# Attention and two MLPs on one core: the first two pairs of heads issued in the written order, the first weight read from GpSimd's queue

## The chip, the cores and the metric

One core of a Trainium2 chip runs the kernel. Its engines are TensorE (PE in the profile: matrix products into PSUM), VectorE (DVE), ScalarE (ACT), GpSimd (POOL) and SyncE (SP, which here only issues DMAs). Each issues its own instructions strictly in order and waits on the others by semaphores. The metric is the device time of one execution in microseconds (us). The kernel before takes 930.9 us, the median of three runs (930.15 to 1106.56).

## The reference

Causal attention on 4 batches of 8 heads, 576 positions, head size 64, with a bias from running sums of max(s, 0), then two MLPs on the 2304 tokens of width 512, each up to 2048 and back:

```python
scores = q @ k.T / sqrt(64)
cum = cumsum(max(s, 0)); scores += min(-(cum[:, None] - cum[None, :]), 0)
attn = softmax(where(causal, -1e9, scores)); y = attn @ v
x = y.transpose(0, 2, 1, 3).reshape(2304, 512)
x = max(x @ w1_in, 0) ** 2 @ w1_out
h = x @ w2_in; out = max(0.01 * h, h) @ w2_out
```

## The kernel before, in words

Heads are worked two at a time: a `Pair` holds two heads on the upper and lower 64 partitions, and there are 16 pairs, four to a batch. A pair has seven slots (`STEPS`, line 78): the score tiles of 128 query rows, kinds 0 (tiles 0 and 1), 2 and 3 once for each head, and kind 4, the last 64 rows of both heads. In a slot VectorE takes a tile's scores plus mask from PSUM and reduces them to the row minimum (`maxima`, line 488; on the reversed sign, so it is the maximum), ScalarE takes the exponential with the row sum (line 512), TensorE transposes the result (`flip`, line 527), ScalarE (kinds 0 and 2, line 550) or VectorE (kinds 3 and 4, line 548) copies that out of PSUM as `pT`, TensorE multiplies by the values (`values`, line 569), ScalarE copies the product to `xo` (line 579), and VectorE scales it by the inverse of the sums (lines 585, 586 and 610, with a broadcast `ex` made by GpSimd, line 589, and turned by TensorE, line 604). TensorE makes the scores of a coming tile (lines 469 and 457) as soon as their PSUM banks, tagged `S` and `h`, are free. The next pair's q and k are transposed by VectorE (line 427; from pair 5 on also split into two parts, lines 430 to 432).

Two other streams are laid into these slots. From slot 35 (the start of pair 5) TensorE works on the first MLP's first product (`up1`, line 661, called by `fill`), for blocks of 512 tokens whose attention is done. From slot 11, at the pace of one for 2.5 slots, `load_w` makes the 16 pieces of the first weight ready: a read of 512 KB of "words" by DMA (line 154) into one of two buffers `wst`, two ScalarE steps (lines 114 and 115), two VectorE steps (117 and 120), a sum on GpSimd (122), then the rounded copy (169 on ScalarE, or 171 on VectorE) and the rest on GpSimd (172). Each `yield` ends the part of one slot.

What sets the order: the program is written slot by slot (lines 810 to 867), and a scheduler that plays the program on a clock of its own may issue each engine's instructions in another order, where nothing ties them. `in_order(start, engines)` ties all instructions of the named engines since `start` to the order in which they are written. Before, one such tie covers TensorE from slot 35 to the end; shorter ones cover single groups of TensorE.

Of the kernel before, what the change touches and what calls it, by code (L numbers as in the profile page):

```python
# [18 lines left out]
def f32(ap):  # L19
    return ap.bitcast(F32)  # L20
# [3 lines left out]
def attention_then_two_mlps(  # L24
# [24 lines left out]
    nc = tc.nc  # L49
# [61 lines left out]
    def words(t, st, adder=nc.gpsimd):  # L111

        lw, hw = st[:, :, 0], st[:, :, 1]
        nc.scalar.activation(f32(t), f32(hw), AF.Copy, scale=2.0 ** -112)  # L114
        nc.scalar.activation(lw, lw, AF.Copy, scale=2.0 ** -29)  # L115
        yield
        nc.vector.tensor_scalar(t, t, 0x07FFFFFF, 3, ALU.bitwise_and, ALU.logical_shift_left)  # L117
        if adder is nc.vector:
            nc.vector.tensor_tensor(t, t, lw, ALU.add)  # L119
        nc.vector.scalar_tensor_tensor(t, hw, 0xC0000000, t, ALU.bitwise_and, ALU.bitwise_or)  # L120
        if adder is not nc.vector:
            adder.tensor_tensor(t, t, lw, ALU.add)
        yield
# [25 lines left out]
    def read_w(st, w, ch, rows, queue=nc.sync):  # L149

        if rows:
            queue.dma_start(st.rearrange("p f t -> p (f t)"), w.bitcast(U32)[ch * P:(ch + 1) * P, :])
        else:
            queue.dma_start(
                st.rearrange("p (c f) t -> p c (f t)", c=KC),
                w.bitcast(U32)[:, ch * 2 * P:(ch + 1) * 2 * P].rearrange("(c p) f -> p c f", p=P))

    def load_w(fc, pool, stage, lo_engine=nc.gpsimd):

        st = stage.words()  # L160
        read_w(st, w1_in, fc, False)
        for _ in range(3):
            yield
        dst = pool.tile([P, 2, DM], F32R, tag=f"w{fc}", name=f"w{fc}")
        win[fc] = dst
        t = stage.word()
        yield from words(t, st)
        if fc < 10:
            nc.scalar.activation(dst[:, 0], f32(t), AF.Copy)
        else:  # L170
            nc.vector.tensor_copy(dst[:, 0], f32(t))
        lo_engine.tensor_tensor(dst[:, 1], f32(t), f32(dst[:, 0]), ALU.subtract)
# [143 lines left out]
    def in_order(start, engines):  # L316

        before = {}
        for i in nc.cur_bb.bb.instructions[start:]:
            if i.engine not in engines:  # L320
                continue
            if i.engine in before:
                tc.add_manual_dep(
                    i, before[i.engine].name,
                    mybir.DependencyInfo(mybir.DependencyClass.NoSync, mybir.DependencyReason.DATA),
                    reason="in_order")
            before[i.engine] = i
# [180 lines left out]
    def exponentials(t, m, tiles, sums, c0):  # L508

        for x, (a, z, c) in enumerate(tiles):  # L510
            s0 = c0 + 2 * x
            done = nc.scalar.activation(t[:, a:z], t[:, a:z], AF.Exp, bias=m[:, c:c + 1], scale=-1.0,  # L512
                                        accum_out=sums[:, s0:s0 + 1])
        return done.ins
# [156 lines left out]
    def attention(at, mg, mx):  # L671

        n = len(STEPS)
# [3 lines left out]
        def at_slot(y, f, *args):  # L677
            later.setdefault(y, []).append((f, args))
# [51 lines left out]
        START = [4 * n * (j + 1) + (10 if j else 7) for j in range(B)]  # L730
# [6 lines left out]
        for x in range(len(pairs)):  # L737
            y = n * x
# [18 lines left out]
        stage = Stage(at, at, 2)  # L757
        for fc in range(FC):
            job = load_w(fc, wpool, stage)
            for gap in range(6):  # L760
                at_slot(CV + 5 * fc // 2 + (4 if fc > 7 else 0) + gap, step, job)
        for ch in range(BEFORE):
            job = convert(*divmod(ch, FC), stage, nc.sync, 3)
# [45 lines left out]
        live, anchors = {}, [None, None]  # L809
        for y in range(end + 14):  # L810
            x, st = divmod(y, n)
            if y == START[0]:
                fixed_from = len(nc.cur_bb.bb.instructions)
            if y < end:
                args = maxima(at, x, *STEPS[st])
                live[y] = args[0]
                behind = [args[-1], exponentials(*args[:-1])]
# [357 lines left out]
```

## Time and profile before

| | us |
|---|---|
| median of 3 runs (lowest, highest) | 930.9 (930.15, 1106.56) |
| the profiled execution | 932.79 |
| its span, first to last instruction | 931.0 |
| busy: PE, DVE, ACT, POOL | 898.3, 705.7, 577.7, 179.9 |
| first reduction of pairs 0 to 4 (line 488) | 10.69, 22.63, 34.78, 49.43, 64.81 |
| first product of `up1` (line 661) | 78.70 |

A row of the timeline gives start, duration, engine, line, operation, and in brackets how long the engine stood idle before it and what released it. A row of the windows gives a stretch (start:end), its length, then the busy time and number of instructions of PE, PE's weight loads, DVE, ACT and POOL, the granted clock of TensorE as a share of its full speed, the busy share of the DMA engines, and GB/s. A row of the waits gives who waited for whom, us in total, times, and the longest.

### The profile page before, as it was taken

What the parts mean: (1) busy time and instruction counts of PE and PEld (TensorE: products, weight loads), DVE (VectorE), ACT (ScalarE), POOL (GpSimd) and SP (SyncE); (2) the same over time, 40 slices, a digit from 0 to 9 for tenths busy, and PEclk for the clock granted to TensorE, in tenths of its full rate; (3) what the DMA queues carried; (4) which work ended last, traced back from release to release, by engine and by line L of the source; (5) the groups of instructions that cost most, each with busy time, mean ns of one, the idle gap of its engine ahead of it and who ended that gap; (6) DMA issues with size and microseconds to landing.
All of it is one profiled execution on the core that took longest, in us unless ns stands there. A gap on an engine that the chain in (4) does not pass through costs nothing.

```text
span 931.0 us, 16390 instructions
## 1 busy us (share of the span) xinstructions
PE 898.3 (96%) x5902; PEld 809.0 (87%) x5902; DVE 705.7 (76%) x1286; ACT 577.7 (62%) x1076; POOL 179.9 (19%) x290
## 2 busy tenths in 40 slices
PE   5878999999999999999999999999999999999997
PEld 3646777777777778999999999999999999999997
DVE  5888776876774267589897997787488697886964
ACT  4788876878886444365565556686577754444442
POOL 4357763344330001001112101001110000000000
PEclk9999999999999999999999999999999999999999
DMA  9776849778763377948649326668768575627303
GB/s 164 172 184 153 217 145 230 219 204 245 227 203 106 99 239 274 316 163 269 228 132 363 128 96 201 218 221 304 256 205 299 187 254 149 182 57 208 86 13 55
DMA packets 229569, 178.48 MB, mean 192 GB/s; under 512 B 139600, under 2 KB 206352, under 8 KB 229488
## 3 DMA queue, kind: packets, MB, share of 16 engines
q1 hardware_dynamic: 192568, 105.13, 41.7%
q10 hardware_dynamic: 27048, 38.16, 11.3%
q0 software_dynamic: 9872, 34.15, 10.5%
q8 instruction: 46, 0.75, 0.3%
q14 instruction: 35, 0.29, 0.1%
HBM read 111.25 MB, written 66.13 MB: 191 GB/s over the span
## 4 chain that ended last, share of the span: by engine, by line
PE 53%; issue 13%; DVE 6%; DMA 6%; POOL 1%; ACT 1%; POOLq 0%; ACTq 0%; DVEq 0%; SPq 0%
PE q L877 30%; PE h L661 16%; DVE op L984 3%; PE tr L569 2%; DMA gp<-gscr 2%; PE S L469 2%; PE tr L527 1%; PE S L457 1%; DMA gp<-qscr 1%; DMA wst<-in_moe_w_in_dram 1%; DMA qscr<-post 1%; DVE gp L978 1%; DMA wst<-in_moe_w_out_dram 1%; DVE wt L119 0%; POOL zscr L1046 0%
## 5 line engine op out<-in xcount | busy, mean ns | idle before, releaser
L877 PE MATMUL q<-op,w 128*128 128x384 f32 x3024 | 527.9, 335 | 4.0 <-DVE op L984 2.7
L877 PEld LDWEIGHTS q<-op,w 128*128 128x128 f32 x3024 | 523.7, 188 | 7.9 <-DVE op L984 5.0
L983 ACT ACTIVATE op<-gp 128x768 fp32r<-128x768 f32 x189 | 158.3, 846 | 152.3 <-PE q L877 128.4
L661 PE MATMUL h<-xs,w 128*128 128x512 f32 (+1 forms) x960 | 211.5, 374 | 1.2 <-ACT gs L640 0.8
L984 DVE TENSOR_TENSOR op<-gp,op 128x768 fp32r<-128x768 f32 x189 | 178.0, 953 | 40.6 <-ACT op L983 39.4
L661 PEld LDWEIGHTS h<-xs,w 128*128 128x128 f32 x960 | 163.6, 189 | 38.0 <-issue 6.0
L512 ACT ACTIVATE t<-t,m 128x256 f32<-128x256 f32 (+4 forms) x134 | 76.1, 569 | 44.1 <-DVE m L488 39.2
L488 DVE CUSTOM_DVE_ANT_0 t<-S,mask 128x128 f32<-128x128 f32 (+4 forms) x119 | 49.5, 460 | 43.3 <-PE S L469 28.2
L640 ACT ACTIVATE gs<-h 128x512 f32<-128x512 f32 (+1 forms) x80 | 43.8, 549 | 47.3 <-PE h L661 46.8
L185 POOL DMA_DIRECT2D wscr<-wt x48 | 26.6, 555 | 231.2 <-DVE wt L120 227.4
L950 DVE TENSOR_TENSOR post<-q,post 128x768 f32<-128x768 f32 (+1 forms) x55 | 51.6, 940 | 15.1 <-PE q L877 14.7
L469 PE MATMUL S<-Y 64*128 64x128 f32 (+3 forms) x324 | 42.9, 372 | 14.0 <-DVE Y L427 8.0
L930 ACT ACTIVATE post<-q 128x768 f32<-128x768 f32 (+1 forms) x56 | 43.8, 782 | 12.6 <-PE q L877 12.5
L114 ACT ACTIVATE wt<-wst 128x512 f32<-128x512 f32 x64 | 42.3, 661 | 12.2 <-DMA wst<-in_moe_w_in_dram 5.9
L569 PE MATMUL tr<-pT,v 128*64 128x320 f32 (+3 forms) x384 | 46.8, 387 | 2.5 <-ACT pT L550 2.0
L120 DVE SCALAR_TENSOR_TENSOR wt<-wst,wt 128x512 uint32<-128x512 uint32 x64 | 48.1, 753 | 0.9
L527 PEld LDWEIGHTS tr<-ident,t 64*128 64x128 f32 x720 | 28.6, 140 | 20.5 <-issue 11.3
L910 ACT ACTIVATE post<-post 128x768 f32<-128x768 f32 x36 | 30.4, 846 | 25.5 <-DVE post L950 25.4
L117 DVE TENSOR_SCALAR wt<-wt 128x512 uint32<-128x512 uint32 x64 | 31.7, 496 | 18.2 <-ACT wt L114 18.1
L569 PEld LDWEIGHTS tr<-pT,v 128*64 128x64 f32 x384 | 24.9, 137 | 23.1 <-issue 4.2
L115 ACT ACTIVATE wst<-wst 128x512 uint32<-128x512 uint32 x64 | 42.9, 670 | 2.7 <-DMA wst<-in_moe_w_out_dram 1.8
L198 DVE TENSOR_TENSOR w<-wq,w 128x512 fp32r<-128x512 f32 x49 | 33.3, 688 | 14.2 <-ACT w L197 13.9
(119 smaller groups left out, 943.7 us busy)
## 6 DMA issues: line engine op xcount, KB each, us to landing
gscr<-gs ACTq DMA_DIRECT2D x36, 512.0 KB
gp<-gscr SPq DMA_DIRECT2D x48, 384.0 KB
qscr<-post ACTq DMA_DIRECT2D x48, 384.0 KB
gp<-qscr SPq DMA_DIRECT2D x48, 384.0 KB
wscr<-wt POOLq DMA_DIRECT2D x48, 256.0 KB, 4.5
wst<-in_moe_w_in_dram SPq DMA_DIRECT2D x19, 512.0 KB
wst<-in_moe_w_out_dram SPq DMA_DIRECT2D x16, 512.0 KB
wst<-in_moe_w_out_dram POOLq DMA_DIRECT2D x16, 512.0 KB, 5.1
```

The costliest lines, as they stand in the source:

```text
L120: nc.vector.scalar_tensor_tensor(t, hw, 0xC0000000, t, ALU.bitwise_and, ALU.bitwise_or)
L469: nc.tensor.matmul(p.sc[kind][e][:, a:z], qs[hs, T * P:(T + 1) * P], ks[hs, :z - a], start=(n == 0 and y == 0), stop=(n == len(tiles) - 1 ...
L488: return nc.vector.tensor_tensor_reduce(t[:, a:z], sc, msk, -QK_SCALE, first, ALU.add, ALU.min, m).ins
L512: done = nc.scalar.activation(t[:, a:z], t[:, a:z], AF.Exp, bias=m[:, c:c + 1], scale=-1.0, accum_out=sums[:, s0:s0 + 1])
L569: p.anchor = nc.tensor.matmul(po[64 * e:64 * e + 64, a:n], p.vr[:, c, e], rhs[e], start=(y == 0), stop=(y == len(mm) - 1), skip_group_chec ...
L640: done = nc.scalar.activation(g, h[:, :w], AF.Relu)
L661: nc.tensor.matmul(h[:, :w], win[fc][:, a, c * P:(c + 1) * P], xs[j, c][:, z, :w], start=(c == 0 and y == 0), stop=(c == KC - 1 and y == 2))
L877: i = nc.tensor.matmul(*args, skip_group_check=True, **kw).ins
L930: done = nc.scalar.activation(t[:, xs], acc, AF.Copy)
L950: done = nc.vector.tensor_tensor(t[:, xs], acc, t[:, xs], ALU.add)
L983: a = nc.scalar.activation(t[:, 0], src, AF.Copy)
L984: c = nc.vector.tensor_tensor(t[:, 1], src, f32(t[:, 0]), ALU.subtract)
```

## The change

Three edits. The 16 reads of the first weight's words are issued by GpSimd's queue, not SyncE's. The rounded copy and what follows it move one slot later. And in slots 0 to 13, the first two pairs, TensorE, VectorE and ScalarE are tied to the written order.

```diff
@@ load_w
-        read_w(st, w1_in, fc, False)
+        read_w(st, w1_in, fc, False, nc.gpsimd)
...
         yield from words(t, st)
+        yield
         if fc < 10:
             nc.scalar.activation(dst[:, 0], f32(t), AF.Copy)
@@ attention
-            for gap in range(6):
+            for gap in range(7):
                 at_slot(CV + 5 * fc // 2 + (4 if fc > 7 else 0) + gap, step, job)
...
         for y in range(end + 14):
             x, st = divmod(y, n)
-            if y == START[0]:
+            if y in (0, START[0]):
                 fixed_from = len(nc.cur_bb.bb.instructions)
+            if y == 2 * n:
+                in_order(fixed_from, (nc.tensor.engine, nc.vector.engine, nc.scalar.engine))
```

Behind the 322nd row of VectorE's order and the 142nd of ScalarE's the orders of all engines are the same as before. Line numbers of the new kernel are higher by 1 to 3.

**Place 1, VectorE in pair 0**, right after the four reductions of kind 0. Before:

```order
L585 TENSOR_SCALAR sums<-sums 128x4
L586 RECIPROCAL sums<-sums 128x4
L488 ISA t,m<-h,mask 128x384
L488 ISA m 128x1
L427 STREAM_TRANSPOSE Y<-kr 128x576
L488 ISA t,m<-h,mask 128x384
L488 ISA m 128x1
L427 STREAM_TRANSPOSE Y<-qr 128x576
L488 ISA Y,m<-S,mask 128x512
```

and now:

```order
L489 ISA t,m<-h,mask 128x384
L489 ISA m 128x1
L489 ISA t,m<-h,mask 128x384
L489 ISA m 128x1
L428 STREAM_TRANSPOSE Y<-kr 128x576
L489 ISA Y,m<-S,mask 128x512
L489 ISA m 128x1
L428 STREAM_TRANSPOSE Y<-qr 128x576
L489 ISA Y,m<-S,mask 128x512
L489 ISA m 128x1
L586 TENSOR_SCALAR sums<-sums 128x4
L587 RECIPROCAL sums<-sums 128x4
```

The inverse of the sums (585, 586) moves from ahead of the reductions of kinds 2 and 3 to behind them, and the transposes of the next pair's k and q each move one reduction back.

**ScalarE at the same place**, before:

```order
L512 ACTIVATE t,sums<-t,m 128x384 x2
L512 ACTIVATE Y,sums<-Y,m 128x512
L550 ACTIVATE pT_244<-tr 128x6x64 x2
L512 ACTIVATE Y,sums<-Y,m 128x512
L512 ACTIVATE t,sums<-t,m 128x576
```

and now:

```order
L513 ACTIVATE t,sums<-t,m 128x384 x2
L551 ACTIVATE pT_244<-tr 128x6x64 x2
L513 ACTIVATE Y,sums<-Y,m 128x512 x2
L551 ACTIVATE pT_281<-tr 128x2x3x64 x2
L580 ACTIVATE xo<-tr 128x256
```

The copies of the first turned tiles (`pT`) move ahead of the exponentials of kind 3.

**Place 2, TensorE from pair 0's values to pair 1's first scores** (`S` and `h` are the banks of kinds 0 and 2). Before:

```order
L569 MATMUL tr<-pT_244,v 64x256 x2
L569 MATMUL tr<-pT_244,v 64x128 x2
L527 MATMUL tr<-ident,t 128x64 x11
L469 MATMUL h<-Y 128x384
L527 MATMUL tr<-ident,t 128x64
L469 MATMUL S<-Y 128x128
L469 MATMUL h<-Y 128x384
L469 MATMUL S<-Y 128x128
L469 MATMUL h<-ag_89 128x384
L469 MATMUL S<-Y 128x256
```

and now:

```order
L570 MATMUL tr<-pT_244,v 64x256 x2
L570 MATMUL tr<-pT_244,v 64x128 x2
L528 MATMUL tr<-ident,t 128x64 x12
L470 MATMUL S<-Y 128x128 x2
L470 MATMUL S<-Y 128x256 x2
L470 MATMUL S<-ag_89 128x128 x2
L470 MATMUL S<-ag_89 128x256 x2
L470 MATMUL h<-Y 128x384 x2
```

The scores of kind 0 now stand ahead of those of kind 2, no longer mixed with them.

**Place 3, GpSimd at the start**, where `ident`, `mask` and `ag` are being set up and `aug` is the bias in DRAM. Before:

```order
L330 ISA
L330 AFFINE_SELECT ident<-ident 128x128
L406 MEMSET v 64x128
L331 AFFINE_SELECT mask<-mask 128x128
L348 MEMSET ag_88 4x576 x2
L360 DMA aug<-ka 32x2x576
```

and now:

```order
L331 ISA
L331 AFFINE_SELECT ident<-ident 128x128
L407 MEMSET v 64x128
L154 DMA wst<-in_moe_w_in_dram 128x4x256 x2
L332 AFFINE_SELECT mask<-mask 128x128
L349 MEMSET ag_88 4x576 x2
L361 DMA aug<-ka 32x2x576
```

The first two reads of words are now GpSimd's first DMAs. Each of the other 14 stands in its order behind the sum (122) that last read the buffer.

## Rows read from the trace of the kernel before

**Rows 1.** The windows: stretches between the starts of the pairs.

```profile
10.69:22.63 11.94, 9.44 (x76) 6.29 (x74) 6.31 (x27) 7.56 (x23) 2.45 (x10) 0.86 0.99 180
22.63:34.78 12.15, 10.75 (x123) 7.71 (x121) 9.35 (x36) 8.77 (x26) 2.36 (x9) 1.00 0.63 166
34.78:49.43 14.65, 11.83 (x135) 8.19 (x132) 12.89 (x43) 11.31 (x31) 8.06 (x12) 1.00 0.91 183
49.43:64.81 15.38, 10.89 (x113) 7.72 (x113) 13.57 (x42) 12.58 (x33) 9.59 (x13) 1.00 0.60 171
64.81:78.70 13.89, 11.14 (x102) 7.12 (x102) 13.83 (x43) 10.74 (x30) 7.73 (x9) 0.88 0.81 171
78.70:100.00 21.30, 20.31 (x164) 15.33 (x162) 16.54 (x49) 18.92 (x46) 16.24 (x24) 1.00 0.72 191
100.00:931.00 831.00, 821.37 (x5197) 754.78 (x5195) 626.63 (x1042) 505.13 (x886) 126.27 (x194) 1.00 0.62 194
```

**Rows 2.** The timeline, VectorE in pair 0.

```profile
12.92 0.17 DVE L585 TENSOR_SCALAR sums<-sums 128x4 f32<-128x4 f32 x1 [1.03 <-ACT t L512]
13.22 0.53 DVE L488 CUSTOM_DVE_ANT_0 t<-h,mask 128x384 f32<-128x384 f32 x1
13.67 0.77 DVE L427 STREAM_TRANSPOSE Y<-kr 128x576 f32<-128x576 f32 x1
...
15.51 0.65 DVE L488 CUSTOM_DVE_ANT_0 Y<-S,mask 128x512 f32<-128x512 f32 x1
...
19.27 0.17 DVE L585 TENSOR_SCALAR sums<-sums 128x5 f32<-128x5 f32 x1 [1.41 <-ACT t L512]
22.63 0.29 DVE L488 CUSTOM_DVE_ANT_0 t<-S,mask 128x128 f32<-128x128 f32 x1 [2.95 <-PE S L469]
```

**Rows 3.** The timeline, ScalarE and TensorE in pair 0.

```profile
11.02 0.91 PE L469 MATMUL h<-ag 64*128 64x384 f32 x2
13.79 0.61 ACT L512 ACTIVATE t<-t,m 128x384 f32<-128x384 f32 x1 [0.90 <-DVE m L488]
16.94 0.85 ACT L550 ACTIVATE pT<-tr 128x384 f32<-128x384 f32 x2
17.84 1.07 PE L569 MATMUL tr<-pT,v 128*64 128x256 f32 x8 [2.01 <-ACT pT L550]
19.54 1.65 PE L469 MATMUL h<-Y 64*128 64x384 f32 x4
```

**Rows 4.** The waits: totals, times and longest, first 78.7 us; SyncE's own to 130 us.

```profile
POOL last L442 <- DMA ag<-aug: 14.0, 6, 10.1
...
ACT wt L114 <- DMA wst<-in_moe_w_in_dram: 2.1, 2, 1.5
...
SPq L154 <- POOL wt L122: 13.3, 6, 4.9
```

**Rows 5.** The word reads: on POOL's queue later on; one of SyncE's.

```profile
L154 POOL DMA_DIRECT2D wst<-in_moe_w_in_dram x13: 753/753/763, 353.0 to 521.1; - x13
...
DMA to landing us min/median/max: 4.0/5.4/7.9
...
74.27 0.37 SPq L154 DMA_DIRECT2D wst<-in_moe_w_in_dram  x1
```

**Rows 6.** The timeline: GpSimd ahead of the bias stores, and VectorE beside GpSimd.

```profile
6.91 0.71 POOL L360 DMA_DIRECT2D aug<-ka  x1 [2.50 <-DVE ka L354]
...
61.84 2.50 POOL L172 TENSOR_TENSOR w<-wt,w 128x512 fp32r<-128x512 f32 x2
63.28 1.60 DVE L618 TENSOR_TENSOR xs<-xh,xs 128x512 fp32r<-128x512 f32 x1
...
72.40 0.68 DVE L618 TENSOR_TENSOR xs<-xh,xs 128x512 fp32r<-128x512 f32 x1
```

**Rows 7.** DMA queues: the microseconds 7 to 8 and 28 to 29.

```profile
q1 hardware_dynamic: 250, 0.04, 22.4%
...
q1 hardware_dynamic: 388, 0.38, 107.8%
```

## The prediction

> **What bounds the kernel now.** I read the windows first [rows 1]. From 100 us to the end TensorE is busy 821.4 of 831.0 us, and from 78.70, where the first product of `up1` starts, 20.3 of 21.3. So the last 852.3 us (931.0 - 78.70) are TensorE's work in a fixed order, with hardly a gap to win; the three edits leave that order alone from slot 35 on. Ahead of 78.70 no engine is full in pairs 0 and 1: VectorE is busy 6.3 of 11.9 us and 9.4 of 12.2, so these pairs are as long as the chain from scores to reduction to exponential and back. In pairs 2 to 4 the weight's words come in, and VectorE is busy 12.9 of 14.7, 13.6 of 15.4 and 13.8 of 13.9: there it is nearly the bound itself. What the change can win must therefore come off the start of `up1`, and each us won there is one off the end, as long as TensorE stays full behind it.
>
> The timeline of pair 0 shows its gaps [rows 2, 3]. VectorE stands 1.03 us ahead of the inverse of the first sums, which waits for ScalarE's exponentials, while the `h` scores (ready at 11.02 + 0.91 = 11.93) could have been reduced. It stands 1.41 us ahead of the second inverse, and 2.95 us ahead of pair 1's first reduction at 22.63. That last wait is TensorE's: it stood 2.01 us for `pT`, which ScalarE had copied only at 16.94, behind an exponential of kind 3.
>
> **The change part by part.**
>
> *Pair 0 in the written order.* VectorE ends its first four reductions at 12.92 - 1.03 = 11.9. By the new order two 384-wide reductions follow (0.53 each, to 13.0), k's transpose (0.77, to 13.8), a 512-wide reduction (0.65, to 14.4), q's transpose (to 15.2) and the second 512-wide one (to 15.9). ScalarE has both 384-wide exponentials (0.61 each and a read) done by about 14.1 and copies `pT` (0.85) by 14.9, where it ended at 17.8 before. TensorE then does values (1.07), the next turning and, at 16.7 to 17, pair 1's first scores, now with the kind 2 scores behind them. Before, values to the first reduction took 22.63 - 17.84 = 4.8 us, of which 1.65 was mostly those kind 2 scores and more was lost in mixing; I take 4.0 from 14.9. The bank those scores need is free at 15.9, so it does not bind. Pair 1's first reduction comes at about 19.0 in place of 22.63: a gain of 3.6. Bounds: 1.03, if only the wait ahead of the inverse goes and the other two return elsewhere, and 5.4, the sum of the three gaps.
>
> *Pair 1.* It starts while pair 0's tail is not yet done: VectorE's copies of pair 0's last `pT` now stand between pair 1's first reductions and wait there for TensorE. The inverse that stands ahead of pair 2's first reduction stayed there and waits for ScalarE as before. GpSimd's rows for the bias end at about 26.5, since SyncE issues without a break up to there (the 10.1 us wait [rows 4]), and that time doesn't move. I give back 0.6 here (0 to 1.6): pair 2 starts 3.0 us earlier, near 31.8.
>
> *Word reads off SyncE.* SyncE stood 13.3 us for line 122 alone ahead of line 154 [rows 4], with the v, bias, q and k loads of later pairs queued behind. These loads now go out when their own buffers are free. Most are early anyway; who waited for one was GpSimd's copy of bias rows (14.0 us in 6 waits, 10.1 of it the one above). I take 0.5 (0 to 1.5, a part of the other 3.9).
>
> *Word reads on GpSimd.* Each costs its engine 0.753 us [rows 5]; 16 make 12.0 us, of which the first two, 1.5 us, fit into the 2.50 us in which GpSimd waits for the running sums ahead of the bias stores [rows 6]. Six more fall ahead of 78.70, the last at 74.27 [rows 5], 4.5 us, in a stretch where GpSimd is busy 8.1 of 14.7, 9.6 of 15.4 and 7.7 of 13.9 [rows 1]: room, but its instructions stand in order, and the sum, the rest and the bias rows behind each read come that much later. On the other side a read is issued as soon as line 122 has ended. Landing took 4.0 to 7.9 us from POOL's queue [rows 5], and ScalarE waited for words 2.1 us in two waits ahead of 78.70 [rows 4]. I take a loss of 0.5 (a gain of 1.0 to a loss of 4.5, the reads' whole time on the path).
>
> A rule speaks against this edit. What the row shows: 13 reads of just these words on POOL's queue took 753 to 763 ns, the longest as the shortest, while VectorE was busy beside them [rows 5]. The Trainium skill, SBUF — State Buffer, section "Who interferes with whom", says that GpSimd shares a pair of ports with VectorE, that a VectorE instruction in a two-port mode locks GpSimd out for all its time, and that a DMA issued from GpSimd then waits because its descriptors can't be written. By that rule each read would be stretched and the sum would be a loss; by the row it is 0.753 flat. I go by the row, and keep the lock as a rival.
>
> *The first two reads early.* They move 1.05 MB from about 26 us to about 5. Such a read fills the engines at 0.38 MB in a us [rows 7], so 2.8 us of all DMA work, taken out of a stretch where nobody waits for it. In the new place the engines are at 22% from 7 to 8 us [rows 7] and carry the second head's k, which is wanted at 13.0. Taken as 0; a loss of at most 1.0, if the bias stores behind them in GpSimd's queue push back the bias loads and with them SyncE's row.
>
> *Rounded copy one slot later.* The first weight is needed at 78.70; the first piece is read at slot 11 and now finished in slot 17 in place of 16, still 18 slots ahead of slot 35. Later pieces come one for 2.5 slots, the products use one for about two, and piece 15, done in slot 58, is not needed before slot 60 or so of a block that ends at slot 65. I cost it at nothing; what hides it is that lead. Its gain is that ScalarE need not stand for GpSimd's sum, and that is small.
>
> The sum for the profiled execution: 3.6 - 0.6 + 0.5 - 0.5 = 3.0 us off 932.79 (span 931.0 off to 928.0). The median of the runs shown is 930.9, 1.9 below that execution, and the forecast is made for it: 930.9 - 3.0 = **927.9 us**.
>
> **The rivals.**
>
> *The gain is spent ahead of `up1` (20%).* Pairs 2 to 4 are bound by VectorE's own 40.3 us of work [rows 1], and there the scheduler orders freely; a gain of 3 us in pairs 0 and 1 can be lost in one or two of VectorE's waits of about a us, like those for the sums. For it: 15.4 us of pair 3 with 1.8 idle. Against: a bound of work starts earlier when its first work comes earlier. Time 930 to 931.5.
>
> *GpSimd becomes the bound, slower (13%).* From 78.70 to 100 it is busy 16.2 of 21.3 us [rows 1]; four reads fall there, 3.0 us, which makes 19.2, 90%. There it also makes the split of the next pairs' q and k, without which TensorE's scores, and behind them everything in its fixed order, stand. From the point where its remaining 2 us of gaps can't be closed each read costs its 0.753 us: 8 reads behind 78.70 make 6.0, and 930.9 - 3.0 + 6.0 = 933.9. Against: those gaps are waits for VectorE and ScalarE that the reads can fill.
>
> *The port lock (5%).* In this kernel a two-input instruction of VectorE took 1.60 us beside GpSimd's line 172, as against 0.68 for the same operation from 72.40 on [rows 6], so the two engines do hold each other up. If each of the six reads ahead of 78.70 costs such 0.92 us, that is 5.5: 930.9 - 3.0 + 5.5 = 933.4. The rule above is this one. The 13 unstretched reads [rows 5] speak against it.
>
> *More is won (12%).* With SyncE free and the words issued at once, the 3.6 us in which VectorE stands in pairs 2 to 4 (1.8, 1.8 and 0.1 [rows 1]) may go as well: 930.9 - 3.0 - 3.6 = 924.3.
>
> **How the numbers follow.** My forecast, 925.5 to 930, has 50%. The range reaches to the case where the gain is spent and to the first half of the larger gain: 923 to 932.5, about 8 in 10; what lies above is GpSimd as the bound and the lock. A change of 2% is 18.6 us, about what a measurement of this kernel can tell from none. TensorE's idle time between 10.69 and 78.70 is some 14 us and the dearest mishap costs 6, so none of the cases comes near: within 2% 97%, faster 1%, slower 2%.
>
> **What will show it.** In the trace of the changed kernel pair 1's first reduction stands at 18.5 to 19.5 and pair 2's at 31 to 32.5, with no wait of VectorE ahead of the first inverse and none of 2 us of TensorE for `pT`. The first `up1` product starts at 75 to 76.5, and from there to the end are still about 852 us. GpSimd has 16 rows of 0.75 us, and SyncE no row that waits for line 122. I am wrong if the pair starts are early and `up1` is not (the gain is spent), if the tail is over 853 (GpSimd or the lock; then TensorE waits for `Y`), or if q, k or bias rows of the first two pairs are waited for by VectorE (the early megabyte).

## The result, and the profile after

The changed kernel takes **939.9 us** (median of 6 runs, 936.88 to 942.14) against 931.41 of before: a ratio of 1.0086 [1.0058, 1.0114]. One of before's six runs, at 1106.56 us, was in a slower state and is not in the ratio. The kernel is slower by some 8 us where 3 us less were forecast, within 2% but outside the range. The profiled execution took 940.88 us with a span of 939.1, 8.1 more than before's span. All line numbers behind 167 stand one or more higher than before.

The windows of the changed kernel, as in [rows 1]: six stretches from pair start to pair start (the fifth ends at the first `up1` product), and the rest from pair 6 on, where [rows 1] parts at 100.00.

```profile
14.28:22.62 8.34, 8.34 (x64) 5.20 (x62) 6.05 (x24) 6.39 (x22) 1.52 (x6) 1.00 1.00 169
22.62:35.38 12.76, 11.14 (x132) 7.84 (x128) 9.77 (x38) 8.81 (x28) 2.38 (x9) 1.00 0.47 105
35.38:49.93 14.55, 11.66 (x112) 7.69 (x108) 13.12 (x44) 11.28 (x31) 7.84 (x13) 1.00 0.88 154
49.93:69.02 19.09, 14.21 (x138) 9.29 (x138) 15.06 (x42) 12.45 (x34) 12.98 (x17) 0.91 0.62 172
69.02:80.78 11.76, 10.52 (x102) 6.91 (x102) 11.70 (x39) 11.24 (x30) 6.14 (x10) 0.85 0.70 141
80.78:106.00 25.22, 21.64 (x162) 16.44 (x160) 18.85 (x49) 18.81 (x44) 19.05 (x25) 0.93 0.60 170
106.00:939.00 833.00, 822.03 (x5199) 755.19 (x5197) 626.48 (x1045) 505.45 (x887) 132.22 (x200) 1.00 0.63 194
```

Against [rows 1] three things stand out. Pair 0 takes 8.34 us instead of 11.94, and TensorE is busy through all of it; but it *begins* at 14.28 instead of 10.69, so pair 1 starts at 22.62 as before (22.63). Pair 3 takes 19.09 instead of 15.38. And pair 6 begins at 106.00 instead of 99.63, 6.4 us late. TensorE's work from there on is the same to 1 us (822.0 busy, as against 821.4 from 100 us on), but pair 6 still loses 2 us; the first row is of the changed kernel, the second of before:

```profile
106.00:128.25 22.25, 21.63 (x175) 16.49 (x174) 15.34 (x43) 17.00 (x41) 17.78 (x21) 1.00 0.80 191
99.63:119.81 20.18, 20.18 (x169) 15.36 (x168) 15.27 (x42) 16.39 (x40) 13.71 (x16) 1.00 0.77 198
```

At pair 15 the whole 8.1 us are there (294.93 against 286.82). The first `up1` product comes at 80.78 where 75 to 76.5 was forecast, and from it to the end are 858.3 us, over the 853 that the prediction named as a sign of being wrong.

The forecast for the tie shows in VectorE's timeline of pair 0, which answers to [rows 2]; the added row is ScalarE's copy of `pT` [rows 3].

```profile
14.28 0.29 DVE L489 CUSTOM_DVE_ANT_0 t<-S,mask 128x128 f32<-128x128 f32 x1 [4.88 <-PE S L470]
...
18.77 0.87 ACT L551 ACTIVATE pT<-tr 128x384 f32<-128x384 f32 x2 [1.09 <-issue]
...
22.62 0.29 DVE L489 CUSTOM_DVE_ANT_0 t<-S,mask 128x128 f32<-128x128 f32 x1 [1.22 <-PE S L470]
```

The waits of 1.03, 1.41 and 2.95 us ahead of the inverses and of pair 1 are gone; the longest that is left in the pair is one of 1.22. What is new is the 4.88 us at the head. The timeline of the first 15 us shows where it is from; columns as in [rows 2].

```profile
2.77 1.77 POOL L154 DMA_DIRECT2D wst<-in_moe_w_in_dram  x2
3.83 4.08 SPq L394 DMA_DIRECT2D kr<-in_k_dram  x4
4.55 0.46 POOL L332 TENSOR_SCALAR_AFFINE_SELECT mask<-mask 128x128 bf16<-128x128 bf16 x1
4.97 1.40 POOL L349 MEMSET ag<- 4x576 f32 x2
8.04 2.59 SPq L358 DMA_DIRECT2D ag<-ka  x2
13.35 0.79 PE L470 MATMUL S<-ag 64*128 64x128 f32 x4 [2.23 <-DMA qr<-in_q_dram]
```

And the same in the kernel before:

```profile
2.77 0.28 POOL L331 TENSOR_SCALAR_AFFINE_SELECT mask<-mask 128x128 bf16<-128x128 bf16 x1
3.01 1.40 POOL L348 MEMSET ag<- 4x576 f32 x2
3.83 2.12 SPq L393 DMA_DIRECT2D kr<-in_k_dram  x4
6.08 1.24 SPq L357 DMA_DIRECT2D ag<-ka  x2
9.74 0.80 PE L469 MATMUL S<-ag 64*128 64x128 f32 x4
```

Without a dependence to hold them the first two word reads leave at 2.77 us, ahead of everything that pair 0 waits for. Their issue takes GpSimd 1.77 us, so the mask and the constant (-1) rows of `ag` come 1.8 to 2.0 us later. The four short k loads take SyncE's queue 4.08 us instead of 2.12, the rows `ag` leave at 8.04 instead of 6.08, and TensorE's score product for them, pair 0's last input, runs at 13.35 instead of 9.74. (Its row names the load of q as what released it; the last semaphores that TensorE waits for there are those of the two transfers that leave at 8.04.)

The DMA queues in the microsecond from 5 to 6 (packets, MB, busy share), first in the changed kernel, then before; q0 is GpSimd's queue, q1 SyncE's; ScalarE's, with 15 and 14 packets, is left out:

```profile
q0 software_dynamic: 45, 0.18, 70.4%
q1 hardware_dynamic: 25, 0.00, 2.0%
```

```profile
q1 hardware_dynamic: 1252, 0.16, 98.4%
```

45 records of 4 KB take 70% of the engines' time and leave the short loads 25 packets where they had 1252; from 4 to 8 us these loads have 1752 packets instead of 3532. The Trainium skill, DMA: Bandwidth & Descriptors, section "Queues, rings and completion order", says that each DMA engine takes turns between the queues that have work, a packet of several descriptors at a time. The trace agrees in that the queue whose packets are large takes the time, 70.4% against 2.0%. It does not show even turns: a run below has 839 packets of the short loads beside 48 smaller records.

The word reads and the waits, as in [rows 4, 5] (the issues over the whole span, then one wait of the first 106 us):

```profile
L154 POOL DMA_DIRECT2D wst<-in_moe_w_in_dram x29: 756/768/1002, 2.8 to 529.2; - x29
...
who waited for it (us, times):
  ACT wt L114: 6.5, 7
  ACT wst L115: 3.8, 2
...
DMA to landing us min/median/max: 3.9/5.1/7.9
```

```profile
POOL last L443 <- DMA ag<-aug: 5.0, 5, 3.4
```

SyncE is free: GpSimd's bias rows wait 5.0 us in 106 instead of 14.0 in 78.7. ScalarE waits 10.3 us for words over the span (6.5 + 3.8; before 5.9 + 0.9), at the head of its own order, in pair 3 (1.92 us at 52.43) and in pairs 6 and 7 (1.92 and 2.44). In the first 106 us it is 3.7 us as against 3.2, so these waits alone do not make the 6.4 us by which pair 6 is late.

### The profile page after: what moved, and what is told of

Read it like the earlier page. It is cut to its first block, busy times and chain, and to the rows that moved or that the text cites. A ratio compares the mean times of both kernels' runs of the same rounds, so it can differ in the third digit from the quotient of the medians.

```text
span 939.1 us, 16404 instructions
## 1 busy us (share of the span) xinstructions
PE 902.1 (96%) x5902; PEld 810.5 (86%) x5902; DVE 707.7 (75%) x1286; ACT 577.2 (61%) x1076; POOL 192.1 (20%) x306
## 4 chain that ended last, share of the span: by engine, by line
PE 59%; issue 9%; DVE 7%; DMA 5%; ACT 1%; POOL 1%; POOLq 0%; DVEq 0%; ACTq 0%; SPq 0%
PE q L880 36%; PE h L662 16%; DVE op L987 3%; PE tr L570 2%; DMA gp<-gscr 2%; PE S L470 2%; PE tr L528 2%; PE S L458 1%; DMA wst<-in_moe_w_in_dram 1%; DVE gp L981 1%; DMA gp<-qscr 1%; DVE gp L979 0%; DMA wst<-in_moe_w_out_dram 0%; DMA xscr<-xo 0%; POOL zscr L1049 0%
## 5 line engine op out<-in xcount | busy, mean ns | idle before, releaser
L641 ACT ACTIVATE gs<-h 128x512 f32<-128x512 f32 (+1 forms) x80 | 43.8, 548 | 47.9 <-PE h L662 47.5
L953 DVE TENSOR_TENSOR post<-q,post 128x768 f32<-128x768 f32 (+1 forms) x55 | 51.6, 940 | 15.4 <-PE q L880 15.0
L117 DVE TENSOR_SCALAR wt<-wt 128x512 uint32<-128x512 uint32 x64 | 34.0, 532 | 25.2 <-ACT wt L114 25.0
L933 ACT ACTIVATE post<-q 128x768 f32<-128x768 f32 (+1 forms) x56 | 43.8, 781 | 12.4 <-PE q L880 12.0
```

Source lines behind the costliest of these rows:

```text
L641: done = nc.scalar.activation(g, h[:, :w], AF.Relu)
L953: done = nc.vector.tensor_tensor(t[:, xs], acc, t[:, xs], ALU.add)
```

## The experiments

Each was timed in five rounds; the kernel before stands at 931.7 to 932.1 in all these groups (17 to 35 runs). Differences below are of medians; the intervals of the ratios reach 1.2 to 2.7 us to either side. The starts of pairs are those of one profiled execution of each kernel.

| kernel | us | ratio to before | start of pairs 0, 1, 3, 4, 6 |
|---|---|---|---|
| before | 932.0 | | 10.7, 22.6, 49.4, 64.8, 99.6 |
| changed | 939.9 | 1.0086 [1.0058, 1.0114] | 14.3, 22.6, 49.9, 69.0, 106.0 |
| order only | 933.59 | 1.0015 [0.9999, 1.0031] | 10.4, 18.3, 47.2, 64.5, 99.6 |
| queue only | 940.05 | 1.0085 [1.0070, 1.0101] | 12.8, 23.2, 49.2, 66.1, 105.0 |
| slot only | 932.38 | 1.0004 [0.9988, 1.0020] | 10.3, 20.7, 47.5, 62.9, 98.0 |
| order and slot, reads on SyncE | 933.09 | 1.0016 [1.0003, 1.0028] | 10.4, 17.2, 46.4, 64.4, 98.3 |
| changed, first two reads on SyncE | 936.72 | 1.0046 [1.0030, 1.0063] | 10.3, 17.1, 46.1, 63.2, 102.0 |

**One part alone.** *Order only*, the tie without the other edits:

> Only the tie to the written order in slots 0 to 13; reads on SyncE, no extra slot. Theory A with C (the rest of the loss comes from the reads on GpSimd): pair 1 starts near 19 us, pair 2 near 32, the first product of up1 3 us earlier, ratio about 0.997. Rival D (the tie makes the scheduler order pairs 2 to 5 worse): pair 1 and pair 2 as above, but the gain is gone by the first product of up1 and the ratio is 1.000 to 1.005.

```diff
-            if y == START[0]:
+            if y in (0, START[0]):
                 fixed_from = len(nc.cur_bb.bb.instructions)
+            if y == 2 * n:
+                in_order(fixed_from, (nc.tensor.engine, nc.vector.engine, nc.scalar.engine))
```

*Queue only*:

> Only the reads on GpSimd's queue, in the scheduler's order of before. Theory A with C: the whole loss and no gain from the tie: pair 0 at 14.3, pair 1 at about 26.2, ratio 1.009 to 1.012. Rival D: only the 3.6 us of the early reads, ratio about 1.004.

```diff
-        read_w(st, w1_in, fc, False)
+        read_w(st, w1_in, fc, False, nc.gpsimd)
```

*Slot only* (the added `yield` and `range(7)`):

> The kernel before with the added slot alone: the rounded copy and the subtraction of each weight stand one slot later. Theory (nobody waits for them; first up1 product at about 78.7): within 0.7 us of before, 931.4 to 932.7. Rival: the weights come later than the up1 products ask for them, 933 to 935, with first up1 product later than 80.

*Order and slot*, with the reads left on SyncE (the changed kernel without its `nc.gpsimd`):

> The tie and the later slot, with the reads on SyncE as before. Theory A with C: as with the tie alone, 2.5 to 3.5 us faster than before, ratio about 0.997. Rival D: the ratio is 1.000 to 1.005, with pair 1 early and up1 not.

The queue alone is as slow as the whole change: +8.1 us. The slot is free (+0.4, and -0.5 on top of the order). The order is 4.3 to 5.4 us ahead at pair 1 and 2.2 to 3.1 at pair 3. At pair 6 nothing is left of it, or 1.3 us with the slot, and these are gone by pair 9 (162.72 against 162.70): +1.1 to +1.6 us in the end where -3.0 was forecast.

One row of the table has a gain that no edit made: *slot only* starts pair 1 at 20.7 instead of 22.6, with VectorE's order of before in pair 0. The difference is TensorE's granted clock, which in pair 0 is 1.00 there and 0.86 before [rows 1]: in before's profile it stood at half, 1.2 of 2.4 GHz, from 18.4 to 21.8, after it had stood 2.01 us idle ahead of 17.84 [rows 3]. Pair 0 of *slot only*, and the four `h` scores that took 1.65 us before [rows 3]:

```profile
10.35:20.74 10.39, 8.39 (x76) 5.65 (x74) 6.30 (x27) 7.45 (x23) 2.28 (x10) 1.00 1.02 181
18.73 0.91 PE L470 MATMUL h<-Y 64*128 64x384 f32 x4
```

Pair 0 takes 10.39 us in *queue only* too, again with a clock of 1.00. So 1.55 of the 11.94 us of before are the clock, and of the 3.6 us by which the changed kernel's pair 0 is shorter the tie made 2.05; where the first two reads are on SyncE it made 2.5 to 3.6 (7.88, 6.89 and 6.82 us).

**The early reads.** *First two on SyncE*:

> The changed kernel with its first two reads of words on SyncE's queue, where they stood before; the orders of TensorE and ScalarE are the same as in the changed kernel. Theory A (the two early reads take the DMA engines from the first q, k and bias rows): pair 0's first reduction is back from 14.28 to about 10.7 us, pair 1's from 22.62 to about 19.0, and the end is about 3.6 us earlier than the changed kernel: ratio to the kernel before about 1.005. Rival B (the start is late for another reason, such as the order tie): pair 0 stays at about 14.3 and the ratio at 1.009.

```diff
-        read_w(st, w1_in, fc, False, nc.gpsimd)
+        read_w(st, w1_in, fc, False, nc.sync if fc < 2 else nc.gpsimd)
```

936.72 instead of 939.9: the two early reads cost 3.2 us, and pair 0 starts at 10.3 again. The counterpart puts only these two on GpSimd's queue in the kernel before:

> The kernel before with one edit: the reads of the first two channels' words are on GpSimd's queue, all others stay on SyncE's; TensorE's and VectorE's order is that of before in all pairs. Theory: those two reads leave at 2.8 us instead of about 25 and hold back the short loads of q and k and the writes of the score rows by 3.6 us, whatever the order behind them is: pair 0's first reduction at about 14 instead of 10.69, pair 1 at about 23, and since that pair's end is not held by anything else most of it stays: 934 to 936. Rival: pair 0 of before has waits (its first 11.94 us) in which a start that is 3.6 us later partly disappears: 931.5 to 933.

```diff
-        read_w(st, w1_in, fc, False)
+        read_w(st, w1_in, fc, False, nc.gpsimd if fc < 2 else nc.sync)
```

934.72, ratio 1.0034 [1.0017, 1.0052]: +2.7 with before's order; pair 0 starts at 13.4, pair 1 at 23.8 and pair 6 at 101.0. So the loss is no effect of the tie. The last one keeps the reads' place and their 512 pieces each and drops most of their bytes:

> The changed kernel with the first two word reads on SyncE's queue (936.72 us), and at their old place on GpSimd's queue two reads of as many packets (512 each) with a sixteenth of the bytes, into memory that is not used then. Theory (the bytes of the early reads crowd the short loads and the score rows out of the DMA engines): pair 0's first reduction at 10.3 to 11.3, pair 1 at 17 to 18, time 936 to 937.5. Rival (the issue, 1.77 us of GpSimd ahead of the mask and the zeros of the score rows): pair 0 at 12 to 14.3, time 938 to 940.

```diff
+        if fc < 2:
+            small = pool.tile([P, DM, 2], U32, tag=f"w{14 + fc}", name="small")
+            nc.gpsimd.dma_start(
+                small.rearrange("p (c f) t -> p c (f t)", c=KC)[:, :, :32],
+                w1_in.bitcast(U32)[:, fc * 2 * P:fc * 2 * P + 32].rearrange("(c p) f -> p c f", p=P))
...
-        read_w(st, w1_in, fc, False, nc.gpsimd)
+        read_w(st, w1_in, fc, False, nc.sync if fc < 2 else nc.gpsimd)
```

(It is an eighth of the bytes, 128 of each 1024, not the sixteenth that the expectation names, and the constant rows of `ag` are -1, not zeros. In the trace both reads together are 64 records of 2 KB, so the records are fewer as well as smaller.) 936.98, 1.0057 [1.0037, 1.0078], beside 936.72, 1.0046 without them; pair 0 starts at 11.3, pair 1 at 18.9, later than the 17 to 18 expected. From 5 to 6 us its queues read:

```profile
q1 hardware_dynamic: 839, 0.10, 66.9%
q0 software_dynamic: 48, 0.11, 47.2%
```

With nearly the same issue on GpSimd, 1.68 us, the short loads keep two thirds of their packets. Of the 4.0 us by which pair 0 was late about 1.0 stays, with the issue and an eighth of the bytes; the other 3 go with the bytes.

**The other fourteen reads** cost 3.6 us (936.72 against 933.09), and pair 5 is where they show: 24.4 us (77.56 to 102.01) as against 18.0, in a kernel that began the pair 2.8 us later; at pair 6 the difference is 3.7. The timeline of the kernel with the first two reads on SyncE, pair 5:

```profile
87.62 0.66 DVE L117 TENSOR_SCALAR wt<-wt 128x512 uint32<-128x512 uint32 x1 [1.71 <-ACT wt L114]
87.94 1.49 POOL L122 TENSOR_TENSOR wt<-wt,wst 128x512 uint32<-128x512 uint32 x1
88.31 1.67 DVE L120 SCALAR_TENSOR_TENSOR wt<-wst,wt 128x512 uint32<-128x512 uint32 x1
89.91 0.68 DVE L489 CUSTOM_DVE_ANT_0 t<-S,mask 128x512 f32<-128x512 f32 x1
...
93.06 0.77 POOL L154 DMA_DIRECT2D wst<-in_moe_w_in_dram  x1
...
99.18 0.66 ACT L114 ACTIVATE wt<-wst 128x512 f32<-128x512 f32 x1 [2.99 <-DMA wst<-in_moe_w_in_dram]
...
99.88 0.43 DVE L117 TENSOR_SCALAR wt<-wt 128x512 uint32<-128x512 uint32 x1 [3.71 <-ACT wt L114]
...
102.01 0.29 DVE L489 CUSTOM_DVE_ANT_0 t<-S,mask 128x128 f32<-128x128 f32 x1
```

Two things are to be seen. The sum of channel 7, which frees channel 9's buffer, ends at 89.43, but channel 9's read stands in GpSimd's order behind a part of `Y`, copies and the sum of channel 8, and leaves at 93.06, 3.63 us later; ScalarE stands 2.99 us for it, with pair 6 behind. (Two of the expectations below put this read 6 us late, one of them at 95.6. That row is channel 10's read: the semaphore that ScalarE waits for at 99.18 is the one set by the read of 93.06.) And two words' shifts stand ahead of pair 5's first 512-wide reduction, the second beside GpSimd's sum, where VectorE's 0.69 us becomes 1.67. Two stand there in the kernel before as well, whose reduction comes 10.1 us behind the pair's start instead of 12.4. With all reads on SyncE one word stands ahead and one behind:

```profile
87.34 0.42 DVE L117 TENSOR_SCALAR wt<-wt 128x512 uint32<-128x512 uint32 x1
87.80 0.69 DVE L120 SCALAR_TENSOR_TENSOR wt<-wst,wt 128x512 uint32<-128x512 uint32 x1
88.41 0.68 DVE L489 CUSTOM_DVE_ANT_0 t<-S,mask 128x512 f32<-128x512 f32 x1
...
91.22 1.53 DVE L117 TENSOR_SCALAR wt<-wt 128x512 uint32<-128x512 uint32 x1 [1.51 <-ACT wt L114]
```

First I took the late read of channel 9 for all of it and moved channels 7 to 15 back to SyncE:

> The changed kernel with the reads of channels 0, 1 and 7 to 15 on SyncE's queue; those of channels 2 to 6 stay on GpSimd's. With only 0 and 1 moved back it was 936.72. Theory: what GpSimd's queue still costs there (3.6 us against the same kernel with all reads on SyncE, 933.09) is above all one read, that of channel 9: it left at 95.6 us behind an addition, two subtractions and copies, while its buffer was free at 89.4, and ScalarE stood 3 us for it at the head of its order. With that read on SyncE's queue pair 5 takes 18 to 20 us instead of 24.5 and the time is 933 to 934.5. Rival: each read on GpSimd costs a little, by its 0.77 us there: then the five left cost a third, and the nine moved give back two thirds, 934.3, but no wait of ScalarE is seen to vanish; second rival: SyncE's own queue is late there, 936 to 937.

```diff
-        read_w(st, w1_in, fc, False, nc.gpsimd)
+        read_w(st, w1_in, fc, False, nc.gpsimd if 2 <= fc < 7 else nc.sync)
```

938.11, 1.0072 [1.0045, 1.0098]: my theory fell; the second rival is nearest, 1.1 us under the measured time. On SyncE the read of channel 7 left no sooner (80.63, where GpSimd had issued it at 78.67): the sum of channel 5 freed its buffer only at 78.4, in a pair 4 that began 2.6 us later than with the first two reads on SyncE, and then it stood 2.3 us behind SyncE's read of `xh`. The words run two buffers deep, so a late word makes the next but one late. Hence four buffers, the added two in places of weights not yet written:

> The changed kernel with the first two reads on SyncE's queue (936.72 us, of which 3.6 us against the same with all reads on SyncE's queue) and four buffers for the words instead of two: two of them are the places of the last two weights, free until those are written. The steps of the words keep their places on ScalarE and VectorE but for some rows. Theory: what GpSimd's queue costs from channel 2 on is lateness of reads that wait for a buffer and then for GpSimd's turn (channel 9's read left 6 us after its buffer was free and ScalarE stood 3 us for it). With four buffers no read waits for a buffer, the waits of ScalarE for words after 50 us (1.8, 0.9, 0.8 and 3.0 us) fall to under 1 us together, and the time is 932.5 to 934.5. Rival: the cost lies in the order of the word steps and in GpSimd's own time (0.77 us for each read), which four buffers don't touch: 936 to 937.5.

```diff
-        st = stage.words()
+        spare = f"w{12 + fc % 4}" if fc < 12 and fc % 4 > 1 else None
+        st = pool.tile([P, DM, 2], U32, tag=spare, name="wst") if spare else stage.words()
```

934.19, 1.0024 [1.0011, 1.0038], although with free buffers two reads left at 2.77 us again and pair 0 began at 12.9. Up to 110 us ScalarE no longer waits for any word, and the time is in the theory's range. A run below has the same four buffers with all reads on SyncE, 932.39: between these two the queue costs 1.8 us, the early reads included, where with two buffers it costs 6.8 (939.9 against 933.09). Held back:

> As the run with the first two reads on SyncE's queue, the others on GpSimd's, and four buffers for the words (934.19 us; two reads left at 2.77 us there again and pair 0 began at 12.9), but only channels 4 to 11 use the two added buffers, and their reads are held behind the addition of an earlier channel, so that none leaves at the start. Theory (reads late by buffers and by GpSimd's turn cost 3.6 us, early ones 2.6 more): pair 0 begins at 10.3 to 11, and the time is 931.5 to 933.5. Rival (the order of the word steps and GpSimd's time cost it): 935 to 937.

```diff
+        with after(shifted[-1] if spare else None):
+            read_w(st, w1_in, fc, False, nc.sync if fc < 2 else nc.gpsimd)
```

(with `spare` from channel 4 on; `shifted` holds the sums of line 122.) 935.48, 1.0035 [1.0020, 1.0049]: 1.2 us better than two buffers, not 3.6, in the rival's range. But this run did not take the lateness away: ScalarE still waits 1.93, 2.07 and 1.01 us for words between 46 and 83 us, which the run above does not. So it decides little between the two. Then the order, channel 8's word one slot later, with two and with four buffers:

> As the run with the first two reads on SyncE's queue and the others on GpSimd's (936.72 us), with the steps of channel 8's word one slot later, which puts its shift on VectorE behind pair 5's two reductions over 512 columns and not ahead of them; the reads stay on GpSimd's queue, with two buffers. Theory (two words ahead of that reduction cost pair 5 the time): the reduction starts 8 to 10 us after the pair's start instead of 12.4, and the time is 933 to 935. Rival (late reads, GpSimd's time): pair 5 stays at 23 to 24.5 us, time 936 to 937.5.

> The same one slot for channel 8's word in the run with four buffers and no early reads (935.48 us). Theory (order and lateness together are the 3.6 us): 932 to 933.8, pair 5 at 18 to 20 us. Rival (something else of GpSimd's queue, such as its 0.77 us for each read): 935 to 936.

```diff
-        for _ in range(3):
+        for _ in range(4 if fc == 8 else 3):
...
-            for gap in range(7):
+            for gap in range(8 if fc == 8 else 7):
```

935.38, 1.0034 [1.0019, 1.0048], and 934.20, 1.0032 [1.0015, 1.0050]. In the first the reduction starts 8.1 us behind the pair's start as expected:

```profile
79.23 0.29 DVE L489 CUSTOM_DVE_ANT_0 t<-S,mask 128x128 f32<-128x128 f32 x1
...
87.34 0.68 DVE L489 CUSTOM_DVE_ANT_0 t<-S,mask 128x512 f32<-128x512 f32 x1
...
98.86 0.67 ACT L114 ACTIVATE wt<-wst 128x512 f32<-128x512 f32 x1 [2.65 <-DMA wst<-in_moe_w_in_dram]
```

but channel 9's word still waits, and pair 5 stays at 22.6 us. Both times are a little above what the theory allowed and below the rival's. By the medians order gives 1.3, buffers 1.2, both 2.5 of the 3.6; by the ratios (1.0046, 1.0034, 1.0035, 1.0032) both give no more than either. Each alone is no more than five rounds resolve, so how the 3.6 us divide is not shown.

**Where the order's gain went.** With reads on SyncE pair 3 takes 18.0 us instead of 15.4. Its end in the kernel with order and slot:

```profile
57.41 0.45 SPq L154 DMA_DIRECT2D wst<-in_moe_w_in_dram  x1
...
62.37 0.65 ACT L115 ACTIVATE wst<-wst 128x512 uint32<-128x512 uint32 x1 [0.50 <-DMA wst<-in_moe_w_in_dram]
63.61 0.73 DVE L117 TENSOR_SCALAR wt<-wt 128x512 uint32<-128x512 uint32 x1 [1.77 <-ACT wt L114]
64.37 0.29 DVE L489 CUSTOM_DVE_ANT_0 t<-S,mask 128x128 f32<-128x128 f32 x1
```

A word that lands at 62.4 has its shift on VectorE ahead of pair 4's first reduction. If that is what holds the pair, holding more of the order changes nothing, a word one slot later frees it, and so does an earlier read.

> The kernel before with TensorE, VectorE and ScalarE held in the program's order through the first five pairs (not two); reads on SyncE's queue, no slot added. With two pairs held it was 933.59, and pairs 2 to 4 were no faster than before although they began 3 us earlier. Theory: they are held by the words: the shift of channel 5's word stands right ahead of pair 4's first reduction on VectorE and waits for a read that leaves when the buffers let it (landed at 62.4). The program's order has it at the same place, so holding it brings nothing: pair 4 begins at 63.5 to 65, time 932 to 934.5. Rival: it is the scheduler's order within pairs 2 to 4 (later multiplications and word steps pulled ahead of reductions) that gives the gain back; then pair 4 begins by 62 and the time is 928 to 930.5.

```diff
             if y == START[0]:
+                in_order(fixed_from, (nc.tensor.engine, nc.vector.engine, nc.scalar.engine))
+            if y in (0, START[0]):
                 fixed_from = len(nc.cur_bb.bb.instructions)
```

> As the kernel with five pairs held, with one edit more: the steps of channels 2 and 5 stand one slot later in the program, so that the shift of channel 2's word stands behind two first reductions of pair 3 and that of channel 5's behind two of pair 4 on VectorE, not ahead of them; their reads leave at the same place. Theory (a word's step ahead of a pair's first reduction holds the pair until the read has landed): pair 4 begins 1.5 to 3 us earlier than with five pairs held alone, and the time is 1.5 to 3 us less, 929.5 to 931.5. Rival: the words only make the same wait behind the first reductions, since ScalarE has their first two steps at the same place: less than 0.7 us apart from the other kernel.

```diff
-        for _ in range(3):
+        for _ in range(4 if fc in (2, 5) else 3):
...
-            for gap in range(6):
+            for gap in range(7 if fc in (2, 5) else 6):
```

937.90, 1.0072 [1.0044, 1.0101], and 940.30, 1.0092 [1.0070, 1.0115]: both theories fell, and both rivals. The first starts pair 4 at 62.8, then takes 22.9 us for it; the second starts it at 62.2, then takes 26.3. The program's order is not the better one where the words run. The earlier reads:

> The changed kernel with all reads on SyncE's queue (933.09 us; pairs 1 to 3 begin 3 to 5 us earlier than before, and pair 4 at 64.4 as before) and four buffers for the words instead of two. Theory: pair 3 gives the gain back because channel 5's word, whose read waits for a buffer and lands at 62.4, has its shift on VectorE ahead of pair 4's first reduction; with four buffers it has long landed, pair 4 begins at 61.5 to 62.7, and the time is 930 to 931.7. Rival: pair 3 is long by the work that stands in it, not by a wait for the read: pair 4 at 64 to 65, time 932.5 to 934.

> The kernel before with the first two pairs held in the program's order (933.59 us) and four buffers for the words, without the added slot. Theory as for the kernel with the slot: 930 to 932. Rival: 933 to 934. If the slot matters once the reads are early, this kernel and the one with the slot differ by more than 1 us.

> The kernel before with four buffers for the words and nothing else. Its waits of ScalarE for words up to 90 us are 1.51, 0.61, 0.87 and 0.19 us. Theory: they go and about half of them is on the path: 930 to 931.5. Rival: what waits for words there has time: 931.5 to 932.5.

(each with the two lines for `spare` above.) 932.39, 1.0007 [0.9991, 1.0023]; 932.92, 1.0011 [0.9997, 1.0024]; 931.34, 0.9988 [0.9973, 1.0002]. Four buffers win 0.7 in each, which is not told from nothing; the first two miss the theory's range, the third is inside it but not told from its rival. Pair 4 starts at 63.9 and 62.4; the second of these has pair 6 at 96.0, 3.7 us ahead of before, and its profiled span is 929.2, yet the median of its 12 runs is above that of before.

One rival was not tested: the granted clock. Against *slot only*, whose pair 0 ran at 1.00, *order only* is 2.4 us ahead at pair 1, 0.4 at pair 3 and 1.6 behind at pair 4. Its pairs 2 and 3:

```profile
31.94:47.20 15.26, 12.98 (x118) 8.57 (x116) 12.71 (x45) 11.74 (x32) 8.00 (x14) 0.89 0.84 178
47.20:64.55 17.35, 14.11 (x135) 9.51 (x131) 12.65 (x41) 12.46 (x34) 9.40 (x12) 0.80 0.51 149
```

In before both have 1.00, and TensorE is busy 11.83 and 10.89 us [rows 1]. In pair 3 of *order only* TensorE stood 1.99 and 0.76 us idle ahead of 51.80 and 53.52, and its clock was then at half up to 58. Up to 165 us it is at half for 13.6 us in *order only*, 6.8 in before and 6.8 in the run with pair 6 at 96.0. The timed runs point the same way: the three of *order only* with a mean clock of 0.995 or more took 930.6 to 931.4, the six with 0.992 or less 933.3 to 936.4, while before's nine and seven such runs differ by 0.6 us in the mean. Whether the low clock cost the gain, or both come from the same idle stretches, no run separates. The loss of *queue only* is not this: its six runs have 0.990 to 0.998, and the one with 0.998 is its slowest, 941.37.

## Why the prediction was wrong

*Pair 0 in the written order* was right in its chain, and its number met by luck: 8.34 us instead of 11.94 is the 3.6 forecast, but 1.55 of it is the clock. The step read the 1.65 us of the `h` scores as a price of the order, where the same four take 0.91 at full clock. Where the early reads are away pair 1 starts at 17.1 to 18.3, before the 18.5 to 19.5 forecast, and pair 2 at 31.3 to 31.9 (31 to 32.5). *Pair 1* gave back 0.6 in the changed kernel, as forecast, and 1.5 to 2.1 there.

*The sum failed in the step that carried this gain to the end.* "A bound of work starts earlier when its first work comes earlier" did not hold. The rival "the gain is spent ahead of `up1`", 20%, is what the order alone shows: pair 4 at most 0.4 us earlier, and 933.1 to 933.6, 1.1 to 1.6 above before where -3.0 was summed. The prediction priced the three places that it showed, but VectorE's order changes up to its 322nd row, which is in pair 7. What spends the gain stays open. That a word stands ahead of a reduction is seen in the rows; that it is the cause was not shown: a word one slot later made the kernel slower, and earlier reads won 0.7 us, which is not told from nothing. The clock goes with the loss, and was not tested.

*The first two reads early* is the term outside its own bounds: "taken as 0; a loss of at most 1.0", measured 3.2 (2.7 in before's order). The step looked at the microsecond from 7 to 8, where the engines are at 22% [rows 7], and at the time the reads would need for themselves. The reads left at 2.77 and ran into the microseconds from 5 to 7, where the short loads alone fill the engines to 98 and 87% in the kernel before. And the issue was laid into the 2.50 us wait ahead of the bias stores [rows 6], while it stands ahead of the mask and the constant rows of `ag`, which come before that wait. The sign that the prediction gave for it, q, k or bias rows that are waited for, is there.

*Word reads on GpSimd* and *off SyncE*, together 0, measured 3.6, inside the bounds (a loss of up to 4.5 less a gain of 0.5) and not near the value taken. "A read is issued as soon as line 122 has ended" is the sentence that failed: in GpSimd's order other work stands between, 3.63 us in the row above. The rival "GpSimd becomes the bound" put the loss in the right place, behind 78.70, at 933.9, but by GpSimd's own time; it is 19.05 of 25.2 us busy there, 76% as before. What the runs point to is a read's place in line and its buffer: with four buffers the queue costs 1.8 us instead of 6.8. The share of the words' place in the orders that the scheduler made is not shown. With this term 3.6, the early reads 3.2 and the order and slot 1.1, the steps from one kernel to the next add up to the 7.9 us between 932.0 and 939.9.

*The port lock*, 5%: 29 issues took 756 to 1002 ns, median 768, so the reads were not stretched by much, as the row of before said. The Trainium skill, SBUF — State Buffer, "Who interferes with whom", puts such a wait down to VectorE instructions in a two-port mode; whether one ran beside these issues the rows don't show, so they leave its rule untested here. VectorE's steps beside GpSimd's sums did stretch, 0.69 to 1.67, which [rows 6] had shown.

The slot cost nothing, as forecast.

## What to carry to other kernels

A read that no dependence holds starts as early as its queue lets it: ask what else is on the DMA engines in that microsecond, and count bytes against the short loads that the first work waits for. Moving a read to a busy engine's queue puts it behind that engine's instructions; look for the row that frees the buffer and the row that issues the read, and count what stands between, and which read it is, by the order of the reads. A gain at the head of a chain is worth what the next bound leaves of it, so measure the gain alone before adding edits to it. And read the granted clock of a stretch before you put its length down to an order.

## What the runs showed that was not expected

Two reads of 512 KB took the short loads of the other queue from 1252 packets in a microsecond to 25; reads of as many pieces with an eighth of the bytes left them 839. The issue of a read on GpSimd took 0.77 us late in the kernel and 0.84 to 0.89 for the two at the start (1.77 and 1.68 together), whether it carried 512 or 64 KB. The same order of pair 0 took 11.94 us with a mean granted clock of 0.86 and 10.39 with 1.00.
